# A fused scan-and-FFN kernel: unit 0's spread products over four banks, unit 1's C loaded through ScalarE's queue, and four steps' first products ahead of the first second product

## The chip, the core and the metric

The kernel runs on one core of a Trainium2 chip. The metric is device time in microseconds, the median of several runs of the whole kernel. One execution is also recorded by the hardware profiler; all times inside the kernel come from it, counted from the start of its span.

## The reference

Two blocks follow each other: a chunked state-space scan (Mamba-2) and a feed-forward block. All is float32. In the scan, for 4 sequences, 8 heads, 768 positions, 32 channels and a state of 16:

```python
log_a = np.log(np.clip(a, 1e-06, 1.0))
...
    L = np.exp(cum[:, :, :, None] - cum[:, :, None, :]) * causal
    CB = np.einsum('bhin,bhjn->bhij', Cc, Bc)
    y_intra = np.einsum('bhij,bhjd->bhid', CB * L, xc)
    y_inter = np.einsum('bhin,bhnd->bhid', Cc, state) * np.exp(cum)[:, :, :, None]
    state = decay_full[:, :, None, None] * state + np.sum(Bx, axis=2)
...
h = x @ w_in
g = h * np.cos(h)
return g @ w_out
```

The feed-forward block takes 3072 tokens of 256 values, with `w_in` 256 x 2048 and `w_out` 2048 x 256.

## The kernel before

Time is cut into six chunks of 128 positions. For each chunk the scan gives `yT`, the activations turned for TensorE, and 16 steps then do the feed-forward block on all 512 tokens of the chunk: step n takes 256 columns of `w_in` and half of the tokens.

One step is a chain over four engines. `first(n)` (L641) does four products into a bank `hp`. `wind(n)` takes the whole turns off: ScalarE writes `k` (L648), VectorE writes `w` (L650). `gate(n)` is the sine on ScalarE (L655). `gated(n)` multiplies on VectorE into `gT` (L660) and frees `hp`. `second(n)` adds the products with `w_out` into a bank `o` (L704; later chunks use L742). In the loop `second` runs two steps behind `first`.

Weights are not used as they arrive: each of 16 pieces (512 KB each) is rounded. `grade` makes `mag` on ScalarE (L227), clamps it on GpSimd (L228) and makes `last` on ScalarE (L225); `join` does two operations on VectorE (L241, L243) and the last addition on GpSimd (L251). Piece 0 of `w_in` serves steps 0 and 1, piece 1 steps 2 and 3; piece 0 of `w_out` serves `second(0)` and `second(1)`, and so on.

The first chunk is treated apart, as two units of 64 positions, since nothing is there yet to hide its scan. For unit k: `spread_a` (L336) copies decays over the partitions by products, `decays0` (L348) scans them into `lam`, `turn0` (L367, L369, L371) transposes B and C and copies them out of PSUM, `inner` (L395) does C times B into `g`, `weights` (L405) multiplies with `lam` into `m`, and `finish0` does the products `y` (L421, L429, L439), copies them into `yT` (L447, L449) and takes the masked state (L454). For unit 1, `reach0` (L376, L378) scans the decay of the carried state and `weigh_c` (L383) applies it. `clips` (L819 to L826) makes the decays of all later chunks and writes them to DRAM as `a_cut` and `a_all`, from which `load_a` (`arow`, L160) and `load_along` (`along`, L170) read.

The order on each engine is the order of the program's text (the schedule is written by hand), so whatever is written earlier stands earlier in its engine's queue. [...]`pair` gives two pairs ("scan"), and the tags "h" and "o" two banks each; `hp` lives in "h", so the third `first` waits for the first `gated`. `fill` is a product nobody reads.

DMAs are issued by SP in the order of the text, apart from unit 0's C, which ScalarE issues (L125). Completions are counted on eight semaphores used in turn; an issue waits until the earlier user of its semaphore has landed.

Before the change the early part runs: unit 0 up to its `y`, with unit 1's spreads on both sides of it; then `first_step`, with step 0, unit 1 and the second half of the loads; then the loop from step 1.

Of the kernel before, what the change touches and what calls it, by code (L numbers as in the profile page):

```python
# [25 lines left out]
def kernel(  # L26
# [12 lines left out]
    nc = tc.nc  # L39
# [217 lines left out]
    load_bc(1)  # L257
# [13 lines left out]
    ACT.activation(const.tile([P, 1], FP32, name="sine"), quarter, AF.Sin)  # L271
    V.memset(a0z[:, :, 0:1], 0.0)
# [86 lines left out]
    def turn0(k, tps):  # L359

        if k not in turns0:
            cuts[k] = scan.tile([P, 2, 2, P], FP32, tag="cT2", bufs=1, name="cT2")
            turns0[k] = scan.tile([P, 2, 2, P], FP32, tag="turned", bufs=1, name="turned0")
        of = [tps[0][:, 0:2], tps[-1][:, -2:]]
        for w in range(2):
            for p in range(2):
                PE.transpose(of[w][:, p], bcs[k][:, w, p].rearrange("p h n -> p (h n)"), ident)  # L367
        for t in range(2):
            ACT.activation(cuts[k][:, :, t], of[1], AF.Copy, scale=slot[:, t:t + 1])  # L369
        for w in range(2 if k else 1):  # L370
            ACT.copy(out=turns0[k][:, w], in_=of[w])  # L371
# [14 lines left out]
    def inner(k):  # L386

        gs[k] = g = [pair("g") for _ in range(2)]
        bT, cT = turns0[k][:, 0], cuts[k]
        for p in range(2):  # L390
            for s in range(2):
                ss = slice(s * W, (s + 1) * W)
                for q in range(4):
                    r = slice(32 * q, 32 * q + 32)
                    PE.matmul(g[q // 2][ss, q % 2, p * P:(p + 1) * P]  # L395
                              .rearrange("p (t i) -> p t i", t=2),
                              lhsT=bT[r, p, ss], rhs=cT[r, p, :, ss], start=True, stop=True,
                              tile_position=(32 * q, s * W), skip_group_check=True)
# [9 lines left out]
    def finish0(k):  # L408
# [42 lines left out]
        new = states.tile([P, 2, 2, 2 * D], FP32, tag="state0", bufs=2, name="state0")  # L451
        for t in range(2):
            ts = slice(t * D, (t + 1) * D)
            ACT.activation(new[:, :, :, ts], y[0][:, :, 3 * P:].rearrange(  # L454
                "p s (q d) -> p s q d", q=2)[:, :, :, ts], AF.Copy, scale=slot[:, t:t + 1])
        states0[k + 1] = new
        if k == 0:
            return
        dec = scan.tile([P, 2, 2, 2 * D], FP32, tag="whole", bufs=1, name="whole")
        r4 = reach1.rearrange("p (q s) i -> p s q i", s=2)  # L460
        for s in range(2):
            G.tensor_tensor(out=dec[:, s], in0=old[:, s],
                            in1=r4[:, s, :, W:].to_broadcast([P, 2, 2 * D]), op=ALU.mult)
        G.tensor_tensor(out=new, in0=new, in1=dec, op=ALU.add)
        for u in range(2):
            state[0, u] = new[:, u].rearrange("p s (t d) -> p s t d", t=2)
# [161 lines left out]
    def first(n, between=None):  # L628
        c, f = divmod(n, NF)
        hp[n] = bank([P, TB], "hp", "h")  # L630

        u, j = turn_of(n)
        if c == 0:
            to_, y = hp[n].rearrange("p (e i) -> p e i", e=2), yT[0][:, u]
        else:
            to_ = hp[n].rearrange("p (e t s i) -> p e t s i", e=2, t=2, s=2)
            y = yT[c].rearrange("p k (u s t i) -> p k u t s i", u=2, s=2, t=2)[:, :, u]
        for e in range(2):
            fs = slice((2 * j + e) * P, (2 * j + e + 1) * P)
            for k in range(KT):  # L640
                PE.matmul(to_[:, e], lhsT=w_in[:, k, fs], rhs=y[:, k],  # L641
                          start=(k == 0), stop=(k == KT - 1), skip_group_check=True)
            if between and e == 0:
                between()
# [164 lines left out]
    finish0(0)  # L809
    spread_a(1, 1, "o")  # L810
    decays0(1, 0)
    decays0(1, 1)
    reach0(1)

# [61 lines left out]
    def first_step():  # L876

        first(0, lambda: turn0(1, [pair("tp")[:, 0].rearrange("p (k i) -> p k i", k=4)]))
        weigh0(1)
        weigh_c(1)  # L880
        inner(1)
        fill(bank([P, 4, P], "warm", "o"), 1)
        for q in range(2):
            weights(1, q)
        wind(0)
        grade("in", 1)
        clips()
        join("in", 1)
        gate(0)
        finish0(1)  # L890
        grade("out", 0)
        gated(0)
        rest = grade(*piece[1], later=True)
        join("out", 0)
        rest()

    first_step()
    rest_of_loads()
    for n in range(1, NC * NF + LAG):
        c, f = divmod(n, NF)  # L900
        if n < NC * NF:
# [16 lines left out]
            if n in piece and n > 1:  # L918
                join(*piece[n])
# [6 lines left out]
            if n < 2:  # L926
                join(*piece[n])
# [56 lines left out]
```

## Time and profile before

| | us |
|---|---|
| median of 3 runs | 377.77 (377.76 to 378.14) |
| the profiled execution, whole time | 377.96 |
| its span | 376.1 |
| TensorE busy | 365.1 |
| VectorE busy | 280.7 |
| ScalarE busy | 173.1 |
| GpSimd busy | 214.3 |

In the profile, PE is TensorE's products, PEld its weight loads, DVE is VectorE, ACT ScalarE, POOL GpSimd and SP the engine that issues most DMAs; a letter q behind a name (SPq) is its queue. L641 is line 641 of the kernel. A float32 product appears as two records of PE and two of PEld, so a step's four products are 8 records. In a timeline, a line gives start, duration, engine, line, operation, what is written and read, the number of instructions merged, and in brackets the idle time of the engine ahead of it with what ended it. "issue" means that nothing the profile shows was waited for.

### The profile page before, as it was taken

The page shows a single profiled execution, that of the slowest core. Times are in us where ns is not written, and L with a number is a line of the kernel's source. Part 1 is how long each engine was busy: PE and PEld are TensorE (multiplying, and loading weights), DVE is VectorE, ACT ScalarE, POOL GpSimd, SP SyncE. Part 2 cuts the span into 40 slices and gives each one's busy share as a digit, 9 for nine tenths or more (in the row PEclk, how much of TensorE's full clock was granted, in tenths as well). Part 3 has the DMA queues.
Part 4 walks back from the last instruction along what each step waited for, and adds up shares of the span by engine and source line. Part 5 has one row for each costly group of instructions (what it writes and reads, how often), then busy time and mean ns, then how long its engine had stood idle before and what let it go on. Part 6 is the DMA issues. An engine that isn't in the chain of part 4 may idle for free.

```text
span 376.1 us, 8692 instructions
## 1 busy us (share of the span) xinstructions
PE 365.1 (97%) x3274; PEld 326.1 (87%) x3274; DVE 280.7 (75%) x471; ACT 173.1 (46%) x295; POOL 214.3 (57%) x336
## 2 busy tenths in 40 slices
PE   7979999999999999999999999999999999999995
PEld 3558887888899899999899998999999989999994
DVE  5759999989889957987767987766887872554553
ACT  3577676444354335344434445434444443444442
POOL 5577564489946545674454693363775344544451
PEclk9999999999999999999999999999999999999999
DMA  8999897315436641744222735211020000010011
GB/s 125 245 252 253 250 215 153 84 14 141 117 84 82 124 108 16 122 115 115 37 53 24 133 96 138 46 22 17 2 40 8 13 17 2 2 29 2 5 25 28
DMA packets 124426, 31.54 MB, mean 84 GB/s; under 512 B 93569, under 2 KB 120289, under 8 KB 124385
## 3 DMA queue, kind: packets, MB, share of 16 engines
q1 hardware_dynamic: 122144, 30.73, 38.0%
q10 hardware_dynamic: 2240, 0.26, 0.5%
q8 instruction: 26, 0.43, 0.5%
q14 instruction: 16, 0.12, 0.1%
HBM read 27.64 MB, written 3.34 MB: 82 GB/s over the span
## 4 chain that ended last, share of the span: by engine, by line
PE 72%; POOL 7%; DVE 7%; SPq 6%; issue 3%; DMA 3%; ACT 1%; DVEq 0%; POOLq 0%; ACTq 0%
PE hp L641 35%; PE o L742 30%; POOL words L679 3%; PE y L580 2%; SPq L110 2%; SPq L125 2%; PE g L538 2%; DMA a_in<-in_a_dram 1%; DVE mag L243 1%; DVE w L650 1%; DVE gT L660 1%; PE y L573 1%; DMA bc<-in_B_dram 1%; POOL gd L685 1%; PE o L704 1%
## 5 line engine op out<-in xcount | busy, mean ns | idle before, releaser
L641 PE MATMUL hp<-yT,w_in 128*128 128x256 f32 x768 | 183.6, 382 | 3.0 <-issue 1.5
L641 PEld LDWEIGHTS hp<-yT,w_in 128*128 128x128 f32 x768 | 139.4, 190 | 22.3 <-issue 4.5
L685 POOL TENSOR_TENSOR gd<-gT 128x256 f32<-128x256 f32 x79 | 59.2, 749 | 99.1 <-DVE gT L660 85.3
L655 ACT ACTIVATE w<-w,quarter 128x512 f32<-128x512 f32 x96 | 69.4, 723 | 79.8 <-DVE w L650 79.8
L648 ACT ACTIVATE k<-hp 128x512 int32<-128x512 f32 x96 | 57.3, 597 | 80.8 <-PE hp L641 80.3
L650 DVE SCALAR_TENSOR_TENSOR w<-hp,k 128x512 f32<-128x512 f32 x96 | 65.5, 682 | 37.8 <-ACT k L648 37.6
L660 DVE TENSOR_TENSOR gT<-hp,w 128x512 f32<-128x512 f32 x96 | 65.3, 680 | 33.9 <-ACT w L655 25.0
L742 PE MATMUL o<-words,gd 128*128 128x128 f32 x474 | 65.8, 275 | 0.0
L742 PEld LDWEIGHTS o<-words,gd 128*128 128x128 f32 x474 | 59.3, 192 | 0.0
L488 DVE TENSOR_TENSOR_SCAN lam<-arow,unit 128x512 f32<-128x512 f32 x40 | 56.6, 1415 | 0.0
L742 PEld LDWEIGHTS o<-w_out,gT 128*128 128x128 f32 x316 | 47.5, 191 | 4.0
L688 POOL TENSOR_TENSOR gd<-gT,gd 128x128 f32<-128x128 f32 x79 | 44.6, 565 | 6.2
L742 PE MATMUL o<-w_out,gT 128*128 128x128 f32 x316 | 48.0, 274 | 0.0
L687 POOL TENSOR_TENSOR gd<-gT,gd 128x128 f32<-128x128 f32 x79 | 44.1, 559 | 6.2
L559 DVE TENSOR_TENSOR m<-g,lam 128x256 f32<-128x256 f32 x80 | 30.9, 416 | 0.5
L704 PE MATMUL o<-w_out,gT 128*128 128x256 f32 x128 | 30.3, 380 | 0.8 <-POOL w_out L251 0.8
L742 PE MATMUL o<-words,gT 128*128 128x128 f32 x158 | 30.6, 275 | 0.0
L742 PE MATMUL o<-w_out,gd 128*128 128x128 f32 x158 | 30.6, 275 | 0.0
L704 PEld LDWEIGHTS o<-w_out,gT 128*128 128x128 f32 x128 | 24.2, 190 | 4.4 <-POOL w_out L251 1.2
L742 PEld LDWEIGHTS o<-w_out,gd 128*128 128x128 f32 x158 | 24.0, 192 | 0.0
L742 PEld LDWEIGHTS o<-words,gT 128*128 128x128 f32 x158 | 24.0, 192 | 0.0
L759 DVE TENSOR_TENSOR sum<-ps,sum 128x256 f32<-128x256 f32 (+1 forms) x27 | 16.7, 644 | 0.6
(104 smaller groups left out, 266.7 us busy)
## 6 DMA issues: line engine op xcount, KB each, us to landing
arow<-a_cut SPq DMA_DIRECT2D x20, 512.0 KB
words<-in_moe_w_in_dram SPq DMA_DIRECT2D x8, 512.0 KB
words<-in_moe_w_out_dram SPq DMA_DIRECT2D x8, 512.0 KB
out_dram<-sum SPq DMA_DIRECT2D x18, 128.0 KB
blocks<-in_B_dram SPq DMA_DIRECT2D x128, 8.0 KB
blocks<-in_C_dram SPq DMA_DIRECT2D x128, 8.0 KB
xr<-in_x_dram SPq DMA_DIRECT2D x14, 128.0 KB
along<-a_all SPq DMA_DIRECT2D x20, 64.0 KB
```

The costliest lines, as they stand in the source:

```text
L488: V.tensor_tensor_scan(out=lam[c, b][:, hs].rearrange("p h i -> p (h i)"), data0=rows_.rearrange("p h i -> p (h i)"), data1=unit[:, b % 2 ...
L559: V.tensor_tensor(out=m_[js, :, :, is_], in0=g_[js, :, :, is_], in1=l_[js, :, :, is_], op=ALU.mult)
L641: PE.matmul(to_[:, e], lhsT=w_in[:, k, fs], rhs=y[:, k], start=(k == 0), stop=(k == KT - 1), skip_group_check=True)
L648: ACT.activation(k, hp[n], AF.Copy, bias=0.25, scale=INV_2PI)
L650: V.scalar_tensor_tensor(out=w, in0=hp[n], scalar=INV_2PI, in1=k, op0=ALU.mult, op1=ALU.subtract)
L655: ACT.activation(cos, cos, AF.Sin, bias=quarter, scale=TWO_PI)
L660: V.tensor_tensor(out=gT[n], in0=hp.pop(n), in1=cos, op=ALU.mult)
L685: G.tensor_tensor(out=d[:, 0:2], in0=g[:, 1:2].to_broadcast([P, 2, P]), in1=g[:, 3::-3], op=ALU.subtract)
L687: G.tensor_tensor(out=d[:, 2], in0=g[:, 0], in1=d[:, 0], op=ALU.subtract)
L688: G.tensor_tensor(out=d[:, 3], in0=g[:, 2], in1=d[:, 2], op=ALU.subtract)
L704: PE.matmul(o[c, u][:, t], lhsT=g[:, 2 * e + t], rhs=w_out[:, 2 * j + e], start=(j == e == t == 0), stop=(j == NJ - 1 and e == 1), skip_gr ...
L742: PE.matmul(at[q], lhsT=a_[q], rhs=w[q], start=(j == 0 and q in starts), stop=(j == NJ - 1), skip_group_check=True)
```

## The change

The operations stay the same in kind and number; their order and some buffers change.

- Unit 0's spread goes into four banks (`wide`, two pairs), one for each half of each p; the last two of the eight products stand behind the four transposes.
- `turn0` transposes C ahead of B, and its copies out of PSUM become functions that the caller places: the two cuts, `take(0)` for B, `take(1)` for C. `finish0` likewise returns `take` (masked state) and `add` (decay of the old state and the sum).
- Unit 1's C is issued by ScalarE behind the sine's table load.
- Unit 1's first spread and the reach product stand ahead of unit 0's `inner`, its second spread behind it; the reach scan stands ahead of unit 0's `weights`.
- `inner` does the first bank of `g` whole, then the second.
- Unit 1's transposes stand directly behind unit 0's `y`; they stood between the halves of `hp(0)`.
- `first_steps` writes steps 0 to 3 by hand: `hp(0)` to `hp(3)`, then `second(0)` and `second(1)`; the loop begins with step 4. The pieces of weights, the copies of the unit matrix and the clips are placed between them.

```diff
@@ -254,7 +254,7 @@
...
-    load_bc(1)
+    load_bc(1, (0,))
...
@@ -269,6 +269,7 @@
...
+    load_bc(1, (1,), nc.scalar)
...
@@ -326,27 +327,30 @@
...
-    def spread_a(k, p, tag="h", parts=1):
...
-        spread[k, p] = ps = bank([P, H, W], "a_ps", tag)
-        for i in range(parts):
-            hs = slice(i * H // parts, (i + 1) * H // parts)
+    def spread_a(k, p, parts=(0,), tile_=None):
...
+        n = 2 if tile_ else 1
+        if (k, p) not in spread:
+            spread[k, p] = [t.rearrange("p (h i) -> p h i", i=W) for t in (
+                [tile_[:, i, 0:H * W // 2] for i in range(2)] if tile_ else
+                [bank([P, H * W], "a_ps", "o")])]
+        for i in parts:
...
-                PE.matmul(ps[s * W:(s + 1) * W, hs], lhsT=those[:, b:b + 1].to_broadcast([P, W]),
-                          rhs=a0s[k][:, hs], start=True, stop=True, tile_position=(0, s * W),
-                          skip_group_check=True)
...
-    def decays0(k, p, parts=1):
+                PE.matmul(spread[k, p][i][s * W:(s + 1) * W],
+                          lhsT=those[:, b:b + 1].to_broadcast([P, W]),
+                          rhs=a0s[k][:, i * H // n:(i + 1) * H // n], start=True, stop=True,
+                          tile_position=(0, s * W), skip_group_check=True)
...
+    def decays0(k, p):
...
-        ps = spread.pop((k, p))
-        for i in range(parts):
-            hs = slice(i * H // parts, (i + 1) * H // parts)
-            V.tensor_tensor_scan(out=lams[k][:, p, hs].rearrange(flat),
-                                 data0=ps[:, hs].rearrange(flat),
+        parts = spread.pop((k, p))
+        for i, ps in enumerate(parts):
+            hs = slice(i * H // len(parts), (i + 1) * H // len(parts))
+            V.tensor_tensor_scan(out=lams[k][:, p, hs].rearrange(flat), data0=ps.rearrange(flat),
...
@@ -358,25 +362,29 @@
...
-        if k not in turns0:
-            cuts[k] = scan.tile([P, 2, 2, P], FP32, tag="cT2", bufs=1, name="cT2")
-            turns0[k] = scan.tile([P, 2, 2, P], FP32, tag="turned", bufs=1, name="turned0")
+        cuts[k] = scan.tile([P, 2, 2, P], FP32, tag="cT2", bufs=1, name="cT2")
+        turns0[k] = scan.tile([P, 2, 2, P], FP32, tag="turned", bufs=1, name="turned0")
...
-        for w in range(2):
+        for w in (1, 0):
...
-        for t in range(2):
-            ACT.activation(cuts[k][:, :, t], of[1], AF.Copy, scale=slot[:, t:t + 1])
-        for w in range(2 if k else 1):
...
+        def take(w):
...
+        def cut():
+            for t in range(2):
+                ACT.activation(cuts[k][:, :, t], of[1], AF.Copy, scale=slot[:, t:t + 1])
+        return cut, take
...
-        V.tensor_tensor_scan(out=reach1.rearrange(flat), data0=ps.rearrange(flat),
-                             data1=lead.rearrange(flat), initial=0.0, op0=ALU.mult, op1=ALU.add)
+        return lambda: V.tensor_tensor_scan(
+            out=reach1.rearrange(flat), data0=ps.rearrange(flat),
+            data1=lead.rearrange(flat), initial=0.0, op0=ALU.mult, op1=ALU.add)
...
@@ -387,15 +395,12 @@
...
+        for p, s, q in ((p, s, 2 * t + q) for t in range(2) for p in range(2) for s in range(2)
+                        for q in range(2)):
...
@@ -448,22 +453,25 @@
+        states0[k + 1] = new = states.tile([P, 2, 2, 2 * D], FP32, tag="state0", bufs=2,
+                                           name="state0")
...
+        def take():
...
+        def add():
...
+        return take, add
@@ -795,30 +801,38 @@
     fill(bank([P, 4, P], "warm", "o"), 1)
     fill(bank([P, 2, P], "warm", "o"), 1)
+    wide = [pair("a_ps") for _ in range(2)]
+    spread_a(0, 0, (0, 1), wide[0])
+    spread_a(0, 1, (0,), wide[1])
+    cut0, take0 = turn0(0, [bank([P, 2, P], "tp", "h") for _ in range(2)])
+    spread_a(0, 1, (1,), wide[1])
+    spread_a(1, 0)
     for p in range(2):
-        spread_a(0, p, parts=2)
-        decays0(0, p, parts=2)
-    turn0(0, [bank([P, 2, P], "tp", "o") for _ in range(2)])
+        decays0(0, p)
+    cut0()
+    take0(0)
+    scan_reach = reach0(1)
+    weigh0(0)
     grade("in", 0, n=2)
-    weigh0(0)
     inner(0)
+    spread_a(1, 1)
+    scan_reach()
     for q in range(2):
         weights(0, q)
-    spread_a(1, 0, "o")
     join("in", 0)
-    finish0(0)
-    spread_a(1, 1, "o")
-    decays0(1, 0)
-    decays0(1, 1)
-    reach0(1)
+    take_s0, _ = finish0(0)
+    for p in range(2):
+        decays0(1, p)
     la = const.tile([RB, NU, P], FP32, name="la")
     cut = const.tile([RB, NU, P], FP32, name="cut")
-    def clips():
+    def units_of_decay():
         G.tensor_copy(out=unit[:, 0:HH * P].rearrange("p (h i) -> p h i", h=HH),
                       in_=ident.unsqueeze(1).to_broadcast([P, HH, P]))
         G.tensor_copy(out=unit[:, HH * P:], in_=ident[:, 0:W])
+    def clips():
         G.tensor_scalar(out=cut, in0=a_in, **clip)
         G.memset(cut[:, :, 0:1], 0.0)
         G.tensor_scalar(out=la, in0=a_in, **clip)
@@ -873,30 +887,65 @@
     block_loads = {NF * (c - 1) - 9 + 8 * u: (c, u) for c in range(2, NC) for u in range(2)
                    if by_blocks(c, u)}
-    def first_step():
-        first(0, lambda: turn0(1, [pair("tp")[:, 0].rearrange("p (k i) -> p k i", k=4)]))
+    AHEAD = 4
+    def first_steps():
+        cut1, take1 = turn0(1, [pair("tp")[:, 0].rearrange("p (k i) -> p k i", k=4)])
+        cut1()
+        take1(0)
+        take_s0()
+        take1(1)
+        first(0)
+        inner(1)
+        weigh_c(1)
         weigh0(1)
-        weigh_c(1)
-        inner(1)
         fill(bank([P, 4, P], "warm", "o"), 1)
         for q in range(2):
             weights(1, q)
+        rest = grade("in", 1, later=True)
         wind(0)
-        grade("in", 1)
+        rest()
+        units_of_decay()
+        take_s1, add_s1 = finish0(1)
+        join("in", 1)
+        first(1)
+        gate(0)
+        rest = grade("out", 0, later=True)
+        gated(0)
+        rest()
+        wind(1)
+        take_s1()
         clips()
-        join("in", 1)
-        gate(0)
-        finish0(1)
-        grade("out", 0)
-        gated(0)
-        rest = grade(*piece[1], later=True)
+        first(2)
+        rest = grade("in", 2, later=True)
+        gate(1)
         join("out", 0)
         rest()
-    first_step()
+        gated(1)
+        wind(2)
+        first(3)
+        rest = grade("out", 1, later=True)
+        gate(2)
+        join("in", 2)
+        rest()
+        gated(2)
+        add_s1()
+        wind(3)
+        second(0)
+        rest = grade("in", 3, later=True)
+        gate(3)
+        join("out", 1)
+        rest()
+        gated(3)
+        second(1)
+        rest = grade("out", 2, later=True)
+        join("in", 3)
+        rest()
+    first_steps()
     rest_of_loads()
-    for n in range(1, NC * NF + LAG):
+    for n in range(AHEAD, NC * NF + LAG):
         c, f = divmod(n, NF)
         if n < NC * NF:
@@ -915,7 +964,7 @@
...
-            if n in piece and n > 1:
+            if n in piece:
...
@@ -923,8 +972,6 @@
...
-            if n < 2:
-                join(*piece[n])
...
```

More of the change, by code (lines that the diff above doesn't have):

```diff
@@ L389, in inner @@
         bT, cT = turns0[k][:, 0], cuts[k]
[L390 to L398, printed above, removed]
+        for p, s, q in ((p, s, 2 * t + q) for t in range(2) for p in range(2) for s in range(2)
+                        for q in range(2)):
+            ss, r = slice(s * W, (s + 1) * W), slice(32 * q, 32 * q + 32)
+            PE.matmul(g[q // 2][ss, q % 2, p * P:(p + 1) * P].rearrange("p (t i) -> p t i", t=2),
+                      lhsT=bT[r, p, ss], rhs=cT[r, p, :, ss], start=True, stop=True,
+                      tile_position=(32 * q, s * W), skip_group_check=True)
     def weights(k, q):
@@ L450, in finish0 @@
                      in_=y[0][:, :, 0:2 * P].rearrange("p s (t i) -> p s t i", t=2))
[L451 to L466, printed above, removed]
+        states0[k + 1] = new = states.tile([P, 2, 2, 2 * D], FP32, tag="state0", bufs=2,
+                                           name="state0")
+        def take():
+            for t in range(2):
+                ts = slice(t * D, (t + 1) * D)
+                ACT.activation(new[:, :, :, ts], y[0][:, :, 3 * P:].rearrange(
+                    "p s (q d) -> p s q d", q=2)[:, :, :, ts], AF.Copy, scale=slot[:, t:t + 1])
+        def add():
+            dec = scan.tile([P, 2, 2, 2 * D], FP32, tag="whole", bufs=1, name="whole")
+            r4 = reach1.rearrange("p (q s) i -> p s q i", s=2)
+            for s in range(2):
+                G.tensor_tensor(out=dec[:, s], in0=old[:, s],
+                                in1=r4[:, s, :, W:].to_broadcast([P, 2, 2 * D]), op=ALU.mult)
+            G.tensor_tensor(out=new, in0=new, in1=dec, op=ALU.add)
+            for u in range(2):
+                state[0, u] = new[:, u].rearrange("p s (t d) -> p s t d", t=2)
+        return take, add
     def weigh(c, b):
@@ L626, in turn_of, with first @@
         return (f % 2, f // 2) if c == 0 else divmod(f, NJ)
-    def first(n, between=None):
+    def first(n):
         c, f = divmod(n, NF)
@@ L642, in first @@
                           start=(k == 0), stop=(k == KT - 1), skip_group_check=True)
-            if between and e == 0:
-                between()
     def wind(n):
```

## The prediction

> **What bounds the kernel now.** I read the shares of the engines first, then TensorE's waits, then the busy time by stretches, then the timeline of the first 28 us.
>
> ```profile
> PE 365.1 (97%) x3274; PEld 326.1 (87%) x3274; DVE 280.7 (75%) x471; ACT 173.1 (46%) x295; POOL 214.3 (57%) x336
> ```
> TensorE is idle for 376.1 - 365.1 = 11.0 us of the span. TensorE's waits name those gaps:
> ```profile
> PE g L395 <- ACT turned L371: 1.6, 2, 1.2
> PE hp L641 <- issue: 1.5, 1, 1.5
> PE hp L641 <- DVE gT L660: 0.8, 2, 0.6
> PE o L704 <- POOL w_out L251: 0.8, 1, 0.8
> PE hp L641 <- ACT yT L447: 0.5, 1, 0.5
> PE y L580 <- POOL m L552: 0.4, 1, 0.4
> ```
> Columns: us in total, times, longest. Busy time by stretches:
> ```profile
> 10.00:20.00 10.00, 9.41 (x260) 5.89 (x259) 8.19 (x14) 5.05 (x12) 5.72 (x11) 1.00 1.05 262
> 20.00:27.14 7.14, 4.43 (x59) 3.16 (x45) 3.05 (x6) 5.22 (x12) 5.80 (x9) 1.00 0.92 265
> 27.14:60.00 32.86, 32.86 (x154) 28.91 (x155) 31.75 (x42) 22.50 (x38) 20.22 (x21) 1.00 0.86 225
> ```
> Columns: length, busy PE, PEld, DVE, ACT, POOL, clock, DMA share, GB/s. From 27.14 TensorE has no gap until 60 us, and DVE is 31.75/32.86 = 97% busy beside it. The changed order is the old one again from step 4 on, so the change can win only ahead of that: by bringing the gapless stretch (and DVE with it) forward. The few later gaps end on engines that move along. The timeline there:
> ```profile
> 11.57 0.52 PE L439 MATMUL y<-xr,sc 64*32 64x64 f32 x28
> 15.13 0.84 ACT L369 ACTIVATE cT<-tp,slot 128x256 f32<-128x256 f32 x2 [1.89 <-PE tp L367]
> 17.29 1.29 DVE L405 TENSOR_TENSOR m<-g,lam 128x512 f32<-128x512 f32 x2 [1.71 <-PE g L395]
> 20.90 2.43 PE L641 MATMUL hp<-yT,w_in 128*128 128x256 f32 x10 [0.46 <-ACT yT L447]
> 24.82 1.56 PE L641 MATMUL hp<-yT,w_in 128*128 128x256 f32 x6 [1.49 <-issue]
> 27.14 1.99 PE L704 MATMUL o<-w_out,gT 128*128 128x256 f32 x8 [0.76 <-POOL w_out L251]
> ```
> Unit 0's y ends at 12.09, yet its successor's C is turned only at 15.13; unit 1's y ends at 20.44; then three gaps lie among hp(1), hp(2) and o(0). The chain of waits gives 1.73 us to a step's hp and 1.73 to its o; hp(4) starts at 32.58, and o(2) at 34.15 in the timeline.
>
> **What the skill says.** *PSUM — Partial Sum Buffer*, "PSUM bank collisions raise a hardware error": two engines on one bank must be kept apart by a semaphore, by bank. The trace agrees: the first scan starts at 6.02, 2.1 us after its first product, when four are done, though it reads two. *DMA: Bandwidth & Descriptors*, "Issuing engines are not separate DMA queues": issuing from another engine saves only issue time; here two C issues take 1.45 us on ScalarE, 1.71 on SP. Its "Latency and other measured facts" gives up to 2 us of HBM access at high load, which I add as an estimate to the time at which bytes have moved. *Runtime: NRT & Kernel Launch*, "Instruction fetch mechanics": instructions come in 16 KiB blocks of 256 over a DMA queue of the sequencer's. The trace agrees: queue q8 has 26 packets of 0.43 MB, and TensorE's 6548 instructions / 256 = 25.6. The page calls a crossing "mostly hidden"; the gap "issue" 1.5 inside hp(2), with nothing else to wait for and a q8 packet between 22 and 24 us, reads as one that is not.
>
> **The change part by part**, times from the span's start.
>
> (1) Spread products. The tiles get four banks, but in the built order the first scan still waits for the fourth product and the third scan for the eighth, which now stands behind the four transposes (0.66). Scans 1, 2 start at 6.02 as before. C of unit 0 has landed at about 6.5 (SP's B issue at 4.84 took 2.36, not 0.69, waiting for that semaphore), so transposes 6.55 to 7.25, products 7 and 8 to 8.1, scans 3 and 4 (2 x 0.62) from 8.2 to 9.45, against 8.49. If the banks let pairs overlap, up to 0.5 less; I take nothing. Then unit 1's first spread (1.08) and the reach product to 9.6, g to 10.3; on DVE the reach scan (0.67), moved here from 14.92, ends at 10.4 and m (1.29) at 11.7, before 11.0. y (1.09 behind m's end) ends at 12.75: **0.65 lost**.
>
> (2) C of unit 1 from ScalarE. Its second issue waits for unit 0's C (6.5) and costs 0.7: ScalarE is free at 7.25, as its transpose is. SP loses 1.7 us of issue, but the DMA share is about full from 3 to 26 us, so the bytes come no sooner: B and C of unit 1 have moved by about 11.2, landing by 13.2 at worst, wanted at 12.75; x of unit 0 by 8 to 9, landing before 11.1. Cost taken 0, bounds -0.3 and +0.5, should y or the transposes wait.
>
> (3) Order behind y(0). Transposes follow y at once (0.62), ScalarE does yT (0.49 from start to start), cuts from 13.4 (0.73), bT, the masked state copies (0.53), cT to 15.3. hp(0) runs 13.4 to 15.3 beside them. g from 15.3; DVE: m to 11.7, joins (1.45), two scans (2.32) to 15.5; m from 15.65 to 16.95 (before 17.29 to 18.58). The filler product (1.12) ends at about 17.1, y(1) needs 2.0: ends at 19.15 instead of 20.44, **1.3 won**. hp(1) 0.46 later at 19.6, to 21.35. POOL's units copies and min/max fit beneath.
>
> (4) hp(2), hp(3) ahead of o(0). hp has two banks, so hp(2) waits for gT(0). Its sine now stands behind yT(1) on ScalarE: 19.8 to 20.5, gT(0) to 21.2, hidden by hp(1). The block fetch, asked for near y(1)'s start (18.3 there, 17.2 here) and back after 6.4 us, gives 23.6: hp(2) ends at 23.6 + 3 x 0.43 + 0.27 of filling = 25.15. hp(3) waits for gT(1): k 21.65, w to 22.95, join of w_out to 24.4 (0.42 + 0.98), product to 25.05. So hp(3) 25.1 to 26.85, o(0) and o(1) without a gap to 30.3 (the w_out join on POOL is done by 25.7), hp(4) to 32.05: 2.3 ahead.
>
> (5) What is late next: the second w_out piece, for o(2). k(2) waits for hp(2): 25.2 to 25.8; w to 26.5; join on DVE to 27.75; POOL adds that w_in piece to 29.0, then the state's decay and sum, put here (1.57), to 30.6, min/max to 31.2, w_out (1.27) to 32.5. o(2) starts at 32.55 instead of 34.15. gT(4) by the same chain ends at 35.8, before 37.68, so DVE keeps up. **Won on the path: 1.6 us.**
>
> (6) Clips. a_in's clip waits behind min/max of w_out, itself behind the sine: 21.8 instead of 19.25; a_all's write leaves SP at 23.0 instead of 20.60, with chunk 1's B, C, x, along and arow queued behind it on SP. The backlog of weights empties at about 25, so along moves only from 26.75 to 27.4, arow from 27.56 to 28.2. Wanted by DVE at 35.8 (before 37.60); its bytes moved by 31 in the old run. Cost 0; if the cover goes, each us behind 35.8 is one us.
>
> The sum against the profiled execution: 376.1 - 1.6 = 374.5 span, with 377.96 - 376.1 = 1.86 around it 376.36; its 377.96 is 0.19 above the median of 377.77, so **376.2**.
>
> **The rivals.** *A, more is won*: the fetch is early or hidden; hp(2) ends at 23.35, k(2) at 25.1, the chain of (5) is 0.65 shorter and o(2) follows hp(4) at 32.0: 2.15 won, 375.6. For it: the fetch has a changed neighbourhood, as SP is idle from about 16 us. Against: bytes fill the engines until about 25.
>
> *B, hardly anything*: the fetch comes back when the weights' backlog empties, at 24.8 as before, not 6.4 us after its request. Then hp(2) ends at 26.4, (5) shifts by 1.25, o(2) starts at 33.75: 0.4 won, 377.4. For it: the DMA share at 0.92 in that stretch. Against: queues share the engines, and one packet of 16 KB isn't behind all the weights.
>
> *C, slower*: the clips' delay reaches DVE's first scan of arow. One mechanism: a_all's write, needed by along, lands later than 27.4, and arow, behind it on SP, lands behind 35.8. I estimate its landing at 33.6 (31 + 0.6, and 2 for the landing). The win is gone when it lands after 35.8 + 1.6 = 37.4; landing at 38.3 it costs 2.5: 378.7. DVE at 97% couldn't make that good. For it: SP issued arow only at 27.56 in the old run, one us behind a write that left six before. Against: 2 MB of weights followed arow in the old run, and all landed in time.
>
> A fifth outcome, that the change does nothing of what it says, is excluded for the order of hp; for the four banks it is part of the forecast.
>
> **How the numbers follow.** The forecast's own range is 375.8 to 376.8, from the bounds of (1) and (2). Chances: forecast 0.44, A 0.20, B 0.22, C 0.14. Leaving out C and little else gives 375.1 to 378.1. A measurement of this kernel can tell about 0.2% (0.76 us) from no change: faster means below 377.0. Forecast and A nearly all, and a little of B: 0.65; B's rest and a little of C: 0.22; slower 0.13.
>
> **What would show it.** m of unit 1 from about 15.65; y(1) ended near 19.15; four hp before the first o; a gap ahead of hp(3) ended by gT; a short one ahead of o(2) ended by POOL w_out; o(2) at about 32.5; no wait of DVE for arow. Wrong would be: m of unit 0 later than 12.2, an "issue" gap in hp(2) that ends at 24.8, or a DVE idle before the first arow scan.

## The result: no change that can be measured, and the profile after

| | before | after |
|---|---|---|
| median of the same runs (4 each) | 377.76 (377.45 to 378.14) | 377.65 (377.32 to 377.95) |
| the profiled execution, whole time | 377.96 | 377.81 |
| its span | 376.1 | 376.0 |
| VectorE's first scan of an arow starts | 37.60 | 37.84 |

The ratio is 0.9996, with a 95% interval of 0.9979 to 1.0014. The forecast was 376.2. The changed kernel was measured once more later, over 22 runs: 1.0007 (0.9993 to 1.0022) of the kernel before.

Engine shares of the changed kernel, first part of its page (busy us, share, instructions):

```profile
PE 365.3 (97%) x3274; PEld 326.0 (87%) x3274; DVE 281.7 (75%) x471; ACT 172.7 (46%) x295; POOL 215.1 (57%) x336
```
TensorE is idle for 10.7 us of its span, for 11.0 before. So its idle time hardly went; it moved. TensorE's longest waits (us in total, times, longest; one of 1.1 us in front of the first filler product, which the kernel before has too, is left out):

```profile
PE hp L649 <- POOL la L838: 1.9, 1, 1.9
PE o L710 <- POOL w_out L251: 1.2, 1, 1.2
PE hp L649 <- DVE gT L666: 1.1, 3, 0.6
```
The two waits of `g` for ScalarE's copies of the turned B and C (1.6 before: 1.2 in unit 0, 0.4 in unit 1) are gone. The pause in front of hp(2) is longer than before, the one in front of an o has grown from 0.8 to 1.2, and hp waits for gT three times instead of twice. Busy time by the stretches shown before (length, PE, PEld, DVE, ACT, POOL, clock, DMA share, GB/s):

```profile
10.00:20.00 10.00, 9.09 (x276) 6.07 (x273) 7.97 (x13) 5.08 (x14) 5.53 (x10) 1.00 1.10 252
20.00:27.14 7.14, 5.26 (x26) 4.47 (x25) 4.14 (x8) 5.97 (x12) 4.68 (x8) 1.00 0.93 279
27.14:60.00 32.86, 31.48 (x147) 26.96 (x146) 31.28 (x40) 21.56 (x37) 22.50 (x24) 1.00 0.89 230
```
In the middle row TensorE does 0.83 us more than before. In the last, where it had no gap, it is idle for 1.38 us and VectorE is busy 0.47 us less, while GpSimd has 2.28 us more to do. The win of the front is handed back behind 27 us. The timeline shows the place:

```profile
15.95 1.29 DVE L410 TENSOR_TENSOR m<-g,lam 128x512 f32<-128x512 f32 x2 [0.82 <-PE g L401]
23.44 3.61 PE L649 MATMUL hp<-yT,w_in 128*128 128x256 f32 x16 [1.88 <-POOL la L838]
26.89 3.62 PE L710 MATMUL o<-w_out,gT 128*128 128x256 f32 x16
30.34 1.89 PE L649 MATMUL hp<-yT,w_in 128*128 128x256 f32 x8
33.41 1.99 PE L710 MATMUL o<-w_out,gT 128*128 128x256 f32 x8 [1.18 <-POOL w_out L251]
```
Unit 1's m starts 1.34 us earlier than before, and hp(4) at 30.34 instead of 32.42: TensorE is 2.1 us ahead there. (The prediction took 32.58 for the old hp(4) from the chain of waits, which counts a start later than the timeline does.) But o(2) starts at 33.41 instead of 34.15, only 0.74 ahead. GpSimd in between:

```profile
28.11 1.28 POOL L251 TENSOR_TENSOR w_in<-mag,last 128x512 uint32<-128x512 uint32 x1 [0.63 <-DVE mag L243]
29.36 1.39 POOL L469 TENSOR_TENSOR whole<-state,m 128x128 f32<-128x128 f32 x2
30.82 0.73 POOL L471 TENSOR_TENSOR state<-state,whole 128x256 f32<-128x256 f32 x1
31.53 0.61 POOL L228 TENSOR_SCALAR mag<-mag 128x512 f32<-128x512 f32 x1
32.10 1.25 POOL L251 TENSOR_TENSOR w_out<-mag,last 128x512 uint32<-128x512 uint32 x1
```
It works without a pause: the sum of the state (L469, L471) stands ahead of the clamp of the next w_in piece (L228) and of w_out(1), which o(2) waits for. And VectorE, which waits for that clamp:

```profile
32.17 1.48 DVE L241 TENSOR_SCALAR mag<-mag 128x512 uint32<-128x512 uint32 x1 [1.08 <-POOL mag L228]
33.68 0.98 DVE L243 SCALAR_TENSOR_TENSOR mag<-words,mag 128x512 uint32<-128x512 uint32 x1
34.58 0.68 DVE L656 SCALAR_TENSOR_TENSOR w<-hp,k 128x512 f32<-128x512 f32 x1
35.18 1.12 DVE L241 TENSOR_SCALAR mag<-mag 128x512 uint32<-128x512 uint32 x1
36.33 0.98 DVE L243 SCALAR_TENSOR_TENSOR mag<-words,mag 128x512 uint32<-128x512 uint32 x1
37.24 0.68 DVE L666 TENSOR_TENSOR gT<-hp,w 128x512 f32<-128x512 f32 x1
37.84 1.92 DVE L496 TENSOR_TENSOR_SCAN lam<-arow,unit 128x512 f32<-128x512 f32 x1
```
VectorE stands idle for 1.08 us ahead of a join, whose first operation (L241) usually takes 0.42; here it takes 1.48, and in the next join 1.12. In the kernel before, GpSimd did the decay earlier and in 0.76 us (1.39 now), and L241 of the one join between gT(3) and gT(4) took its usual time:

```profile
21.88 0.76 POOL L462 TENSOR_TENSOR whole<-state,m 128x128 f32<-128x128 f32 x2
35.65 0.42 DVE L241 TENSOR_SCALAR mag<-mag 128x512 uint32<-128x512 uint32 x1
37.00 0.68 DVE L660 TENSOR_TENSOR gT<-hp,w 128x512 f32<-128x512 f32 x1
```
So gT(4) ends at 37.92, where before it ended at 37.68, and the first scan of an arow starts 0.24 us later than before. From here on VectorE sets the pace (from 51.3 to 69 us it is busy for 17.4 of 17.7 us, before for 17.5), and the later waits fall at the same times: y's wait for POOL m ends at 100.35, before at 100.46.

An account for VectorE, added up from its timeline between the end of unit 1's m and that first scan, where every kernel of this study runs the same 22 operations (5 w, 5 gT, 6 joins of two operations):

| kernel | m ends | operations | idle | first scan | span |
|---|---|---|---|---|---|
| before | 18.58 | 14.50 | 4.52 | 37.60 | 376.1 |
| after | 17.24 | 15.28 | 5.32 | 37.84 | 376.0 |
| sum late (first experiment) | 17.24 | 15.05 | 4.85 | 37.14 | 375.5 |
| decay twice | 17.07 | 15.30 | 6.36 | 38.73 | 376.9 |
| fewer instructions | 17.22 | 15.32 | 4.22 | 36.76 | 375.0 |
| front alone | 17.08 | 14.50 | 5.49 | 37.07 | 375.1 |
| sum late and fewer instructions | 17.23 | 14.83 | 3.39 | 35.45 | 375.0 |
| sum late, no fillers | 17.21 | 14.83 | 3.44 | 35.48 | 375.1 |

The changed kernel has m 1.34 us earlier, and loses 0.8 us to longer operations and 0.8 us to idle time. The first scan tells the end: in the first six rows the span is 338.0 to 338.5 us longer than its start, and in the last two it is too, once the late waits of 1.3 and 1.4 us that are told below are taken off. The experiments ask which edits cause the losses ahead of the scan.

### The profile page after: what moved, and what is told of

It is laid out like the page before. It is cut to its first block, busy times and chain, and to the rows that moved or that the text cites. A ratio compares the mean times of both kernels' runs of the same rounds, so it can differ in the third digit from the quotient of the medians.

```text
span 376.0 us, 8691 instructions
## 1 busy us (share of the span) xinstructions
PE 365.3 (97%) x3274; PEld 326.0 (87%) x3274; DVE 281.7 (75%) x471; ACT 172.7 (46%) x295; POOL 215.1 (57%) x336
## 4 chain that ended last, share of the span: by engine, by line
PE 71%; POOL 7%; DVE 7%; SPq 5%; DMA 5%; issue 3%; ACT 1%; POOLq 0%; DVEq 0%; ACTq 0%
PE hp L649 34%; PE o L748 30%; SPq L151 3%; POOL words L685 2%; PE y L588 2%; DMA xr<-in_x_dram 2%; PE g L546 2%; DVE mag L243 1%; DVE mag L241 1%; DMA words<-in_moe_w_out_dram 1%; PE y L581 1%; DVE w L656 1%; POOL gd L691 1%; DVE gT L666 1%; SPq L110 1%
```

## The experiments

Three theories, with the letters of the expectations. P: GpSimd's queue is the path, since the state's sum was put ahead of pieces that VectorE and o(2) wait for. F: the pause in front of hp(2), read as a fetch of instructions, is what holds everything behind it. V: VectorE at 97% sets the end whatever else is done. Each ratio below is to the kernel before, run in the same rounds.

**The state's sum later.** The decay and sum of unit 1's state, on GpSimd, go from step 3 to step 11.

```diff
         gated(2)
-        add_s1()
         wind(3)
...
         if n >= LAG:
             second(n - LAG)
+        if n == 11:
+            add_s1()
```

> The decay and sum of unit 1's state (three GpSimd operations, 2.2 us in the changed kernel) move from step 3 to step 11; nothing else changes. Theory P (GpSimd's queue: these operations hold up the clamp of the third w_in piece and the second w_out piece): o(2) starts at about 32.0 instead of 33.41, VectorE has no idle before that clamp's join, its first arow scan starts at about 36.3 instead of 37.84, and the whole takes 1.2 to 1.6 us less than the changed kernel, some 376.2. Theory F (the instruction fetch ahead of hp(2), which makes k(2) and all behind it late): o(2) still near 33, whole within 0.4 us of the changed kernel. Theory V (VectorE's own work bounds from step 0 on): o(2) earlier, but the arow scan within 0.4 us of 37.84 and the whole the same.

Measured: 377.43, ratio 0.9983 (0.9957 to 1.0009), span 375.5. VectorE's timeline at the same join:

```profile
31.24 0.68 DVE L666 TENSOR_TENSOR gT<-hp,w 128x512 f32<-128x512 f32 x1
31.84 1.12 DVE L241 TENSOR_SCALAR mag<-mag 128x512 uint32<-128x512 uint32 x1
```
The idle time ahead of the join is gone, o(2) starts at 32.73 without a wait, and the first scan at 37.14, 0.70 us earlier than in the changed kernel. But in this execution the pause lasted longer (hp(2) at 24.05, not 23.44), so what is won is understated, and in whole time the interval reaches past 1. P is supported by the trace; the whole time alone doesn't show it.

**The decay twice.** The two products of the decay are done twice, so that GpSimd's queue is longer at that place and nothing else changes.

```diff
-            for s in range(2):
+            for s in (0, 1, 0, 1):
                 G.tensor_tensor(out=dec[:, s], in0=old[:, s],
```

> The two products of the state's decay are done twice at their place in step 3 (the second time with the same result). Theory P: the clamp of the third w_in piece, o(2) and the arow scan come 0.8 to 1.4 us later than in the changed kernel, and the whole takes that much more, 378.5 to 379.0. Theories F and V: o(2) later by as much, but the whole less than 0.4 us longer.

Measured: 379.06, ratio 1.0033 (1.0018 to 1.0048), span 376.9. GpSimd's timeline, then VectorE's:

```profile
29.53 2.12 POOL L469 TENSOR_TENSOR whole<-state,m 128x128 f32<-128x128 f32 x4
```

```profile
33.06 1.47 DVE L241 TENSOR_SCALAR mag<-mag 128x512 uint32<-128x512 uint32 x1 [1.80 <-POOL mag L228]
```
The products take 0.73 us more, VectorE's idle time grows by 0.72 (1.08 to 1.80), the first scan starts at 38.73 (0.89 later) and the span is 0.9 longer. Here hp(2) started 0.18 us later than in the changed kernel; the rest, 0.7 us, is the delay of GpSimd's queue, passed on to the scan and the end undiminished, which F alone and V alone don't allow. The whole time rose by somewhat more than the span; 12 of its 20 executions have the lower clock that the last section describes.

**Fewer instructions ahead of the pause.** Unit 1's y is computed without the part that comes from the carried state, so its result leaves that part out. That takes away 16 small products, 64 TensorE instructions; one more filler product (4 instructions) stands in for their time.

```diff
             old = states0.pop(k)
-            for p in range(2):
+            for p in ():
...
-                                  start=(k == p == t == 0), stop=True,
+                                  start=(p == 0) if k else (p == t == 0), stop=True,
...
-        fill(bank([P, 4, P], "warm", "o"), 1)
+        fill(bank([P, 4, P], "warm", "o"), 2)
```

> Unit 1's part of y that comes from the carried state (16 small products, 64 TensorE instructions, 0.98 us) is left out, and one more filler product of 0.85 us with 4 instructions is done in its place, so TensorE reaches its 704th instruction only at o(1). Theory F: the gap of 1.9 us ahead of hp(2) goes, hp(2) starts at about 21.6 instead of 23.44, k(2) at about 24.4 instead of 25.36, and the whole takes about 1 us less. Theory P: the gap goes too, if it is a fetch, but the whole gains under 0.5 us, as the clamp still stands behind the state's sum. If the gap is no fetch, hp(2) still starts near 23.4.

Measured: 376.79, ratio 0.9971 (0.9962 to 0.9980), span 375.0. TensorE's timeline:

```profile
19.49 3.72 PE L649 MATMUL hp<-yT,w_in 128*128 128x256 f32 x16 [0.46 <-ACT yT L452]
24.69 1.97 PE L649 MATMUL hp<-yT,w_in 128*128 128x256 f32 x8 [1.48 <-DVE gT L666]
```
hp(1) and hp(2) run on without a pause, 2.2 us earlier than in the changed kernel, though the same data were loaded by the same transfers and GpSimd's cast of la (L838), which the changed kernel's page names as the releaser, is where it was (22.32 us, for 22.38). The next wait is hp(3) for gT(1). The first scan starts at 36.76, 1.08 earlier; VectorE's idle time at the join stays (1.09), as GpSimd's queue does. So F holds as well as P: two losses, one behind the other.

**Both at once**, the two diffs above together.

> Both edits at once: the state's decay and sum in step 11, and 64 TensorE instructions fewer ahead of hp(2). It leaves out the part of unit 1's y that comes from the carried state. If the two losses are separate (GpSimd's queue holds o(2) and the join; the pause in TensorE holds hp(2)), the gains add: VectorE's first scan of an arow starts at about 36.1 us (37.84 less 0.70 less 1.08) and the span is 374.3 to 374.7 us, 376.1 to 376.5 us by the clock of the runs. If they are one loss seen from two sides, the scan starts at 36.7 us or later and the span is no shorter than the 375.0 us of the kernel with fewer instructions alone.

Measured: 375.88, ratio 0.9945 (0.9926 to 0.9965). The first scan starts at 35.45, earlier than the sum of the two gains gave (36.06), since the longer pause of the first experiment is out of it. The span of the profiled execution is 375.0 all the same, for a late wait that the page of the changed kernel doesn't have: at 183.36 us a product of C and B (L546) has waited 0.71 us for cT, which waits for VectorE's transposes, one of which waits 1.19 us for a later chunk's C to arrive by DMA; an hp behind it waits 0.59. Without them the span would be 373.7; the spans of its other five executions are 373.6 to 374.6, and the median of the whole times is 0.9 under that of fewer instructions alone.

**The front alone.** The changed front up to y(1), then the order of before: the loop from step 1 (`AHEAD = 1`), o(0) behind hp(1) and hp(2), and the state's sum early, ahead of w_out(0).

```diff
-    AHEAD = 4
+    AHEAD = 1
...
         join("in", 1)
-        first(1)
         gate(0)
-        rest = grade("out", 0, later=True)
-        gated(0)
-        rest()
-        wind(1)
         take_s1()
         clips()
-        first(2)
...
+        add_s1()
+        grade("out", 0)
+        gated(0)
+        rest = grade(*piece[1], later=True)
         join("out", 0)
...
```

> The changed early part up to y(1), then the order of before: o(0) behind hp(2), the state's sum ahead of the first w_out clamp. Theory P: the early part's win of 1.3 us at y(1) is kept up to o(0) or partly lost there (o(0) at 26 to 27.1), and the whole takes 0.5 to 1.2 us less than before. Theory F: the fetch ends near 23.4 as in the changed kernel, o(0) about 1.3 us earlier than 27.14, whole 1.2 us less. Theory V: the same as before within 0.4.

Measured: 377.01, ratio 0.9974 (0.9959 to 0.9990), span 375.1, first scan at 37.07. Here VectorE's 22 operations take 14.50 us as before. It was run again beside the changed kernel:

> The changed front alone again, beside the changed kernel in the same rounds: if the order of hp(2) and hp(3) ahead of o(0) with the state's sum in front of GpSimd's pieces gives back what the front wins, this stays 0.5 to 1.0 us shorter than the changed kernel, a ratio to before of about 0.9975; if the earlier gain was a spread of single executions, both have the same ratio.

> The changed kernel itself, for the comparison beside the other two of these rounds: span 375.5 to 376.2 us, the first scan of an arow at 37.5 to 37.9 us, no measurable difference from before.

Measured: front alone 0.9979 (0.9968 to 0.9991), the changed kernel 1.0007 (0.9993 to 1.0022); the two intervals don't meet. So the front wins about 0.25%, and the new order behind it gives that back: hp(3) ahead of o(0), with the pieces and the sum that come with it (hp(2) stands ahead of o(0) in every kernel here, the one before too). The span of the changed kernel's profile in these rounds was 377.7, outside what was expected; the last section shows why.

**The front alone with the sum late.**

> The changed front up to y(1), the order of before from there on (hp(1) and then o(0), no hp ahead), and the state's decay and sum in step 11. If GpSimd's queue is what o(0) waits for in the front-alone kernel (0.98 us), o(0) starts about 0.9 us earlier, near 25.7 us, unless the pause in TensorE (up to about 23.7 us, then hp(2) for 1.7 us) sets it, which allows 25.5; the first scan of an arow starts at 36.2 to 36.6 us and the span is 374.2 to 374.7 us. If VectorE sets it instead, the scan starts at about 37.0 us and the span stays at 375.1 us.

Measured: 377.50, ratio 0.9983 (0.9964 to 1.0003), first scan at 37.57. o(0) no longer waits for w_out(0), but starts at 26.75, since hp(2) took 3.15 us at a lower clock in that execution. This lower clock (last section) divides the executions: the 14 with a mean clock under 0.997 have a median of 377.57, the other 8 one of 376.00 (375.48 to 377.55), where the same choice gives 377.00 for the front alone in the same rounds and 377.77 for the kernel before. So the median says little of the order, and at full clock the later sum is worth some 1 us to the front alone, with the pause left as it was. That is what P says.

**Where the pause stands.** Two kernels shift the instruction count: one without the three filler products (12 TensorE instructions fewer), and one with the last filler cut into smaller ones (16 more).

```diff
-    fill(bank([P, 4, P], "warm", "o"), 1)
-    fill(bank([P, 2, P], "warm", "o"), 1)
...
-        fill(bank([P, 4, P], "warm", "o"), 1)
```

```diff
-        fill(bank([P, 4, P], "warm", "o"), 1)
+        fill(bank([P, 2, P], "warm", "o"), 1)
+        fill(bank([P, 1, P], "warm", "o"), 4)
```

> The changed kernel without its three filler products: 12 TensorE instructions fewer ahead of hp(2). If the pause hangs on a place in the instruction stream, it now falls inside hp(2), after its third product of four: hp(2) begins at about 21.3 us behind hp(1) and one product is left for the end of the pause at about 23.4 us, so hp(2) ends at about 23.9 us instead of 25.1, and o(0) starts 0.5 to 1.0 us earlier, near 26.0 us. If the pause hangs on a transfer or on POOL's cast of la, as the trace's label has it, hp(2) still begins whole at about 23.4 us. In either case GpSimd's pieces and the state's sum stand where they stood, so o(2) stays at 33.2 to 33.4 us and the first scan of an arow at 37.5 to 37.8 us: span 375.6 to 376.0 us, no measurable gain.

> The changed kernel with the filler ahead of y(1) cut into smaller products: 16 TensorE instructions more for about the same time. If the pause hangs on the place in the instruction stream, it now falls ahead of hp(1) instead of hp(2): hp(1) starts only when the fetch is back. If the fetch's return is set by the DMA backlog, that is at 22.5 to 23.4 us, hp(1) and hp(2) then run on to about 26.9 us, gT(1) comes 1 to 2 us later, and the kernel is 0.5 to 1.5 us slower than the changed kernel. If the return moves with the instruction, hp(1) starts at about 21.8 us and the loss is under 0.5 us. If the pause hangs on anything else, hp(1) starts at 19.6 us as in the changed kernel and nothing changes.

Measured: 377.56 without fillers, ratio 1.0000 (0.9981 to 1.0018); 381.95 with more instructions, 1.0109 (1.0080 to 1.0139). TensorE's timeline without fillers:

```profile
19.75 3.50 PE L649 MATMUL hp<-yT,w_in 128*128 128x256 f32 x15 [0.46 <-ACT yT L452]
24.15 0.48 PE L649 MATMUL hp<-yT,w_in 128*128 128x256 f32 x1 [0.90 <-issue]
```
and with more instructions:

```profile
19.70 0.48 PE L649 MATMUL hp<-yT,w_in 128*128 128x256 f32 x1 [0.46 <-ACT yT L452]
23.50 5.19 PE L649 MATMUL hp<-yT,w_in 128*128 128x256 f32 x15 [3.31 <-issue]
```
In the changed kernel 8 of the 16 records of hp(1) and hp(2) come before the pause; with 12 instructions fewer 15 do, with 16 more only one. The whole time of the second is longer than expected by some 3 us; about 1.7 of it is the lower clock of the last section. By two records for four instructions, 14 and none would be expected; the place is met to one record. The pause is tied to a place in the instruction stream, and a few instructions decide whether it hits half a product or two whole steps. Its end hardly moves with them: 23.44 in the changed kernel, 24.15 and 23.50 here.

The packets of q8, which the prediction read as TensorE's queue of instructions, tell what ends it. Each trace has one that starts between 20 and 22.5 us:

| kernel | packet starts | ends | pause ends |
|---|---|---|---|
| before | 22.42 | 23.37 | 24.82 |
| after | 20.89 | 21.96 | 23.44 |
| no fillers | 21.97 | 22.92 | 24.15 |
| more instructions | 20.91 | 22.02 | 23.50 |

In all twelve profiled executions with such a pause it ends 1.2 to 1.5 us after this packet has, in the kernel before too, where both are later. The traces don't name what a packet holds, but with the place in the stream this leaves little room for another cause than a fetch of instructions. It comes back at a time of its own, and the instruction count only decides how much work waits for it. Why its packet starts when it does stays open. The first scan moved to 37.15 without fillers, more than expected (37.5 to 37.8), yet that execution's span of 377.3 holds the late wait for cT as well (1.34 us at 185.64, and 0.59 behind it), and the whole time shows no gain.

**The front alone without fillers.**

> The front-alone kernel without the three filler products. If the place in the instruction stream holds, the pause falls behind the third product of hp(2) here as well, o(0) starts at about 25.7 us if w_out(0) allows (it waited 0.98 us for it with hp(2) ended at 25.4), so nothing or up to 0.5 us is won: first scan of an arow at 36.6 to 37.1 us, span 374.6 to 375.1 us. If TensorE's clock needs the fillers, the clock of the first slices is below 1 and y(0) ends later than 12.6 us, with the span above 375.5 us.

Measured: 378.80, ratio 1.0019 (0.9994 to 1.0044). The clock of the first slices is 1, and the pause falls where it was expected. But o(0) starts at 26.72 with 2.02 us of waiting for w_out(0) (the front alone: 26.61, with 0.98): there GpSimd's piece sets o(0), not the fetch, and a shorter pause doesn't bring it forward. The whole time says less: o(0) itself took 3.65 us at a lower clock (1.99 in the front alone), and 11 of the 14 executions have a mean clock under 0.997.

**Both losses made smaller at once.** The changed kernel with the sum in step 11 and without the three fillers, by the diffs above.

> The changed kernel with the state's decay and sum in step 11 and without the three filler products, so that both losses are made smaller and nothing of the computation is left out. If the gains add, the first scan of an arow starts at 36.3 to 36.6 us (37.15 without fillers, less 0.70 for the sum), the span is 374.6 to 375.0 us where no late wait on VectorE's block transposes (0.7 to 1.3 us near 184 us) comes in, up to 376.3 us where it does, and the median lies 0.5 to 1.2 us under the kernel before. If the pause and GpSimd's queue are one loss, the scan stays at about 37.1 us and the median at about 377.4 us.

Measured: 376.00 (375.73 to 377.90), ratio 0.9958 (0.9941 to 0.9974), span 375.1. Its TensorE:

```profile
19.54 3.50 PE L649 MATMUL hp<-yT,w_in 128*128 128x256 f32 x15 [0.46 <-ACT yT L452]
23.63 0.48 PE L649 MATMUL hp<-yT,w_in 128*128 128x256 f32 x1 [0.59 <-issue]
...
31.70 1.89 PE L710 MATMUL o<-w_out,gT 128*128 128x256 f32 x8
...
183.46 0.91 PE L546 MATMUL g<-cT,turned 32*64 32x256 f32 x32 [0.80 <-ACT cT L530]
```
The pause holds half a product, o(2) starts at 31.70 behind hp(4) without a wait, and the first scan at 35.48. So it is faster than both kernels. The scan is 2.1 us ahead of the kernel before; 0.80 and then 0.59 us of it are lost at 183 us in the execution shown. This is the gain that the forecast had promised. In the changed order it takes both repairs: alone, each leaves an interval that reaches 1. But the front alone with the sum late has the same 376.00 in its 8 executions at full clock, so hp(3) ahead of o(0) isn't shown to add anything; none of the 11 executions here has the lower clock, and 14 of 22 there do.

## Why the prediction was wrong

Its steps (1) to (4) held. (1) y(0) ended at 12.54, for 12.75, in part by luck: m of unit 0 ended 0.57 us before its forecast of 11.7, as scans 3 and 4 started at 7.70 and not at 8.2, and y(0) then waited 0.25 us for x, which step (2) had expected before 11.1. (2) No wait for C shows. (3) m of unit 1 started at 15.95, for 15.65, and y(1) ended at 19.11, for 19.15. (4) hp(2) began at 23.44, for a fetch back at 23.6, and hp(4) at 30.34, right behind o(1), for 30.3. (6) No scan of an arow waited for its data.

**The step that failed is (5)**, in two places. The first is a term of its sum. The state's decay and sum were put at 1.57 us and took 2.19 (29.36 to 31.55): the two products of the decay took 1.39 and not 0.76, with VectorE's join beside them. And the w_in piece ahead of them ended at 29.39, for 29.0; of these 0.39, 0.15 is the forecast's own sum, which gives a join 1.25 us here and 0.42 + 0.98 in (4). So o(2) started at 33.41, for 32.55.

The second place, which decided the time, is the sentence that gT(4) ends at 35.8 "by the same chain", "so DVE keeps up". It ended at 37.92, 2.12 later. The prediction shows no working for VectorE here. The clamp behind the state's sum, which it has ending at 31.2, also releases VectorE's join, and w(4) and gT(4) stand behind this join in VectorE's order; so its 35.8 leaves 4.6 us from that clamp to the end of gT(4). The clamp ended at 32.14, 0.94 late, with VectorE idle for 1.08 us in front of it. Then VectorE took 5.78 us, 1.18 more than the 4.6: in the changed order two joins lie between gT(3) and gT(4), where before one did, and L241 took 1.48 and 1.12 us in them, each time with a GpSimd addition (L251) beside it. The two experiments on the sum show where the wait comes from: moved away, the wait is gone; made 0.73 longer, it grows by 0.72. That the joins were longer because of GpSimd's additions is read from the traces (last section), not tested by itself. With the sum moved and the pause short, in the last experiment, gT(4) ended at 35.56.

The prediction named "a DVE idle before the first arow scan" as a sign of being wrong; that is what came, if from another releaser than the arow it had in mind. Of the rivals, B gave nearly the right time (377.4) for a wrong reason: the fetch was back at 23.44, not 24.8. C didn't happen.

The pause of theory F was forecast rightly in step (4) and is no part of the miss. But the prediction took it as given. The changed order puts it in front of a whole hp, where before 10 of the 16 records of hp(1) and hp(2) had passed, and 12 instructions fewer would have left half a product for it.

## What to carry to other kernels

When a step moves ahead on one engine, follow each of its instructions to everyone that waits for it: here GpSimd's sum was followed step by step to TensorE's o, and the engine that sets the end, VectorE, which waits for the next instruction in the same queue, got half a sentence. Before adding a win up to the end, list the operations that the bounding engine must do between two fixed points, and account for their idle time and their length apart. And where a pause has "issue" as its cause, or a releaser that changes from run to run, count the instructions ahead of it and look for a packet in the queue of instructions, before looking for a transfer of data.

## What the runs showed of the hardware

**A join of VectorE waits out an addition of GpSimd.** L241 takes 0.42 us where no GpSimd operation was under way at its start. In each case read here where it started while GpSimd's L251 ran, it ended 0.28 to 0.30 us after that one's end: in the changed kernel at 33.65 (L251 ended at 33.35) and 36.30 (36.01), in the first experiment at 32.96 (32.67), in the front alone at 29.98 (29.70). So it took 1.48, 1.12, 1.12 and 1.12 us, by how early it started, not by its size. *SBUF — State Buffer*, "SBUF: two separate sides", says that VectorE, in some forms of operation, and GpSimd take a pair of ports in turn, locked for a whole instruction. The traces agree with "the other fully blocks" for this pair of operations. So L241, ready 0.07 us after an addition of 1.25 us had begun, took 1.06 us more than its 0.42.

**A lower clock after the pause, in some executions.** In the later rounds the changed kernel's profile shows it, by stretches of 2 us (the last three columns are the clock, DMA share, GB/s; in the stretches on both sides the clock is 1.00):

```profile
24.00:26.00 2.00, 2.00 (x7) 1.57 (x7) 0.80 (x2) 0.65 (x2) 1.88 (x2) 0.59 0.92 142
26.00:28.00 2.00, 2.00 (x7) 1.59 (x6) 0.32 (x1) 0.95 (x2) 0.00 (x0) 0.56 0.51 72
```
hp(2) and hp(3) then take 5.30 us instead of 3.61, and the span is 377.7 instead of 376.0. The four profiles with such a stretch near 24 us (this one, front alone again, front with sum late, more instructions) have pauses of 2.1 to 3.3 us ahead of it; a fifth (front alone without fillers) has it from about 27 us, behind its wait of 2.02 us. The four in which the pause was absent or at most 0.9 us long don't have it. But the first profile of the changed kernel (1.88), the sum late (2.50), the decay twice (2.23) and the front alone (2.34) have the pause without it. *TensorE: Matmul & The Clock Gate*, "What's actually happening", has the clock fall to half after a window of some 3.4 us of idle time, and come back after a busy window of the same length; the traces agree in the rate and in the way back: taken by stretches of 1 us, the middle of it has a clock of 0.50 in all five profiles, and what it lacks comes to 1.7 us of full clock in each (0.41 + 0.44 of 2 us each above), so to 3.4 us at half. But a pause of 2.1 us was enough here, in some executions and not in others. What decides it stays open.

It doesn't touch the result: the four executions of the changed kernel compared there have a mean clock of 0.997 or more, for 0.993 in the profile with such a stretch. It does touch the medians of some later runs. A mean clock under 0.997 is recorded for 8 of the 22 later executions of the changed kernel, 10 of 22 of the front alone beside it, 14 of 22 with its sum late, and for none of the kernels with fewer instructions or of the last one. Without these executions the changed kernel's median is 377.83, the front alone's 377.00 and that of the kernel before 377.77, so the order of the three stays.

**One pause, four names.** The same pause in front of hp(2) is put down to "issue", to POOL la L838, to POOL mag L228 and to POOL state L471 in four executions, by what GpSimd happened to end last.
